# Reordering the superblocks of a fused attention, gated-convolution and MLP kernel

## The chip, the core and the metric

The kernel runs on one core of one Trainium2 chip. The metric is device time in microseconds (us), from the start of the program to its end. Engines are named as in the profile: PE is the matmul engine, PEld its weight loads, DVE the vector engine, ACT the scalar engine, POOL GpSimd, SP the engine whose queue issues all DMAs of this kernel.

## What is computed

Three layers in a row, all in float32, on 8 x 576 rows of 512 values: attention inside chunks of 64 rows (8 heads of 64), a block whose value projection is gated by the sigmoid of a 5-tap causal convolution, and an MLP with a layer norm ahead of it and a residual:

```python
attn = softmax(q_c @ k_c.T / sqrt(64));  x = attn @ v_c          # per chunk and head
gate = sigmoid(sum(conv_w[k] * shift(x, 4 - k) for k in range(5)))
x = (gate * (x @ w_val)) @ w_out
xn = (x - mean(x)) / sqrt(var(x) + 1e-6) * g_ln
out = x + maximum(xn @ w_ch1, 0) @ w_ch2                         # 512 -> 2048 -> 512
```

## The kernel before, in words

A float32 operand is cut into a high part and a low part that PE multiplies at full rate; a product is then three matmuls, high x high, high x low, low x high. ACT makes the high part with a copy, and DVE or POOL makes the low part with a subtraction (`high_low`, L475; `relu` in `ff_pair`, L618).

**Attention (about 0 to 260 us).** Units of 256 rows (`NU` = 18). `load_qk(u)` (L78) brings q and k of a unit into one of two buffers, `sc(u)` (L164) makes its scores and at its end loads unit u + 2. The prologue also calls `load_qk(0)`, `(1)` and `(2)` (L664 to L672); `sc(0)` then loads unit 2 a second time into the other buffer, and it is this copy that `sc(2)` reads.

**MLP, first block (about 260 to 400 us).** 512 rows, 16 slices of 128 hidden values: `ff1` makes a slice, `ff2(0, f)` adds its share to four accumulators, in an order written out by hand for PE. Meanwhile the rows of the next 1024 are normalised (`ln_rows`, L404), transposed (`turn_rows`, L427), and turned into the seven right operands of a Strassen product (`right_operands`, L535).

**MLP, four superblocks of 1024 rows (about 400 to 1084 us, `NS` = 4).** A superblock has eight pairs (`NPR`) of hidden slices. `ff_pair` (L596) makes a 2 x 2 block product from seven products (`prod`) in the two PSUM banks `zy` and `x`. A product is 6 matmuls. ACT copies `zy` out (`copy`), DVE adds `x` to the copy (`add`), and four Relus, named by (slice, half), give the tiles `h`. The second matrix of the MLP is applied one pair later: eight *fillings* (`ff2_tile`, L569), 6 matmuls each, stand between the products of the following pair. Fillings 0 to 3 read `h` (0,0) and (1,0) and add into four accumulators over all pairs; fillings 4 to 7 read (0,1) and (1,1), and DVE adds each to `yt` at once. PE's order in a pair is: product 0 (`zy`), 1 (`x`), fillings 0 to 2, product 2 (`zy`), 3 (`x`), filling 3, product 4 (`zy`), fillings 4 and 5, product 5 (`x`), fillings 6 and 7, product 6 (`x`). Relu (1,0) reads `x` after product 6; product 1 of the next pair overwrites `x`.

In the first superblock `make_pair` (L502) also makes the left operands of the next pair, seven parts with four sums on DVE, a copy on ACT and a subtraction on POOL for each part, and writes them to DRAM (`wc`); later superblocks fetch them into a ring of six tiles. In the first pair the only filling is `open_rest` (L960): the last slice of the first block's `ff2`, after which the pools of the superblocks open. In pairs 2 to 5 of the first three superblocks the rows of the next superblock are normalised, and eight transposes follow the pair.

**What sets the order.** On PE the program's order holds in all of this. On ACT, DVE, POOL and SP the compiler's scheduler orders the instructions when the kernel is built: by program order among those that are ready, in its own model of time; on the chip each queue then runs strictly in that order.

## Time and profile before

| | before |
|---|---|
| time, median of 3 runs | 1086.06 us (1085.44 to 1088.45) |
| profiled execution, its own time | 1085.96 us |
| span of the profile | 1084.2 us, 16824 instructions |
| mean granted clock of PE | 0.992 of full |
| PE busy | 1050.2 us, 97% |
| PEld busy | 857.8 us, 79% |
| DVE busy | 672.2 us, 62% |
| ACT busy | 499.4 us, 46% |
| POOL busy | 60.2 us, 6% |
| DMA | 156.31 MB, mean 144 GB/s |

The span is the time from the first to the last profiled instruction; the execution's own time has 1.8 us around it. Busy time is a sum over one engine's instructions. Matmuls are pipelined and their ends are modelled, so that a row of six matmuls reads 1.52 us while the next group starts 1.36 us after it; a short stall of PE is therefore read from starts, or from the waits of the weight loads, and not from PE's busy share. The page's chain of work that ended last is 85% PE.

### The profile page before, as it was taken

How to read it: one execution, taken by the hardware profiler on the slowest of the kernel's cores; microseconds unless marked ns; L12 is line 12 of the kernel's file. 1: busy time of each engine (PE TensorE's matmuls, PEld its weight loads, DVE VectorE, ACT ScalarE, POOL GpSimd, SP SyncE). 2: the span in 40 equal slices, each digit the busy share in tenths (PEclk: the TensorE clock that was granted, in tenths of full speed). 3: DMA queues.
4: the chain of work that ended last, by engine and by line, in shares of the span. 5: the costliest groups of instructions: out<-in, count | busy, mean ns of one | idle time of the engine just before them, and what ended most of it. 6: DMA issues, size and time to landing. Idle time of an engine off the chain costs nothing.

```text
span 1084.2 us, 16824 instructions
## 1 busy us (share of the span) xinstructions
PE 1050.2 (97%) x6778; PEld 857.8 (79%) x6778; DVE 672.2 (62%) x1098; ACT 499.4 (46%) x872; POOL 60.2 (6%) x88
## 2 busy tenths in 40 slices
PE   4899999999999997999999999999999999999998
PEld 4578888888787886888878888887888888888887
DVE  5899999997958884555566344357344438333434
ACT  5777776766858754254432234333233423222211
POOL 1300000000000033222100000000000000000000
PEclk9899999999989999999999999999999999999999
DMA  9534434412389835334427334325432324522202
GB/s 382 215 134 157 146 135 151 147 60 79 136 264 312 289 133 197 114 120 155 156 93 237 98 97 136 99 96 181 149 114 100 102 84 142 188 80 95 86 31 78
DMA packets 58724, 156.31 MB, mean 144 GB/s; under 512 B 5758, under 2 KB 13974, under 8 KB 56214
## 3 DMA queue, kind: packets, MB, share of 16 engines
q1 hardware_dynamic: 58646, 155.23, 41.4%
q8 instruction: 53, 0.87, 0.3%
q14 instruction: 25, 0.20, 0.1%
HBM read 117.46 MB, written 37.75 MB: 143 GB/s over the span
## 4 chain that ended last, share of the span: by engine, by line
PE 85%; DVE 8%; DMA 2%; ACT 2%; issue 1%; POOL 0%; SPq 0%; ACTq 0%; POOLq 0%
PE acc L583 16%; PE x L609 16%; PE psf L583 15%; PE zy L609 10%; PE pso L334 8%; PE psv L334 8%; PE acc L469 4%; PE psh L334 3%; PE sc L174 2%; PE x L249 2%; DVE h L621 2%; DVE cg L303 1%; PE pst L432 1%; PE pst L217 1%; DMA raw<-in_moe_w_ch 1%
## 5 line engine op out<-in xcount | busy, mean ns | idle before, releaser
L629 DVE TENSOR_TENSOR c<-x,c 128x512 f32<-128x512 f32 x96 | 66.3, 690 | 235.1 <-ACT c L625 179.3
L583 PE MATMUL acc<-w,h 128*128 128x512 f32 x768 | 185.4, 391 | 0.0
L583 PE MATMUL psf<-w,h 128*128 128x512 f32 x768 | 184.3, 389 | 0.0
L583 PEld LDWEIGHTS acc<-w,h 128*128 128x128 f32 x768 | 145.1, 189 | 30.5
L583 PEld LDWEIGHTS psf<-w,h 128*128 128x128 f32 x768 | 144.2, 188 | 29.9
L609 PE MATMUL x<-t,wc 128*128 128x512 f32 x576 | 146.5, 390 | 3.4 <-DVE c L629 3.4
L625 ACT ACTIVATE c<-zy 128x512 f32<-128x512 f32 x96 | 58.0, 604 | 186.7 <-PE zy L609 186.6
L609 PEld LDWEIGHTS x<-t,wc 128*128 128x128 f32 x576 | 108.0, 188 | 26.6 <-DVE c L629 4.3
L620 ACT ACTIVATE h<-c 128x512 fp32r<-128x512 f32 x96 | 60.6, 631 | 135.7 <-DVE c L629 135.1
L588 DVE TENSOR_TENSOR yt<-psf,yt 128x512 f32<-128x512 f32 x128 | 88.2, 691 | 23.5 <-PE psf L583 20.7
L303 DVE SCALAR_TENSOR_TENSOR cg<-xf,cw,cg 128x516 f32<-128x516 f32 (+1 forms) x136 | 100.4, 752 | 3.0
L609 PE MATMUL zy<-b,wc 128*128 128x512 f32 x384 | 98.6, 392 | 0.0
L609 PEld LDWEIGHTS zy<-b,wc 128*128 128x128 f32 x384 | 71.2, 188 | 14.2
L621 DVE SCALAR_TENSOR_TENSOR h<-c,h 128x512 fp32r<-128x512 f32 x96 | 68.0, 708 | 13.4 <-ACT h L620 13.1
L334 PE MATMUL pso<-oh,gh 128*128 128x512 f32 x144 | 58.9, 409 | 1.7 <-ACT gh L370 1.7
L477 POOL TENSOR_TENSOR wc<-raws,wc 128x256 fp32r<-128x256 f32 x56 | 45.4, 833 | 247.5 <-ACT wc L476 238.1
L334 PE MATMUL psv<-xh,vh 128*128 128x512 f32 x144 | 58.6, 407 | 0.0
L334 PE MATMUL pso<-oh,gl 128*128 128x512 f32 x144 | 57.4, 399 | 0.8 <-DVE gl L373 0.7
L334 PE MATMUL pso<-ol,gh 128*128 128x512 f32 x144 | 57.1, 396 | 0.0
L334 PE MATMUL psv<-xl,vh 128*128 128x512 f32 x144 | 56.3, 391 | 0.0
L334 PE MATMUL psv<-xh,vl 128*128 128x512 f32 x144 | 56.3, 391 | 0.0
L620 ACT ACTIVATE h<-x 128x512 fp32r<-128x512 f32 x32 | 19.1, 598 | 80.0 <-PE x L609 80.0
(112 smaller groups left out, 1508.7 us busy)
## 6 DMA issues: line engine op xcount, KB each, us to landing
wc<-wc SPq DMA_DIRECT2D x112, 512.0 KB, 3.2
qkr<-in_qk SPq DMA_DIRECT2D x19, 1024.0 KB, 7.1
raw<-in_moe_w_ch SPq DMA_DIRECT2D x32, 512.0 KB, 4.9
vr<-in_v SPq DMA_DIRECT2D x18, 512.0 KB, 4.1
yd<-y SPq DMA_DIRECT2D x36, 256.0 KB, 2.0
out<-yt SPq DMA_DIRECT2D x36, 256.0 KB, 3.6
yr<-yd SPq DMA_DIRECT2D x32, 256.0 KB, 3.7
yt<-yd SPq DMA_DIRECT2D x32, 256.0 KB, 3.6
```

The source lines that it names most:

```text
L174: nc.tensor.matmul(out=ps[CH * c:CH * c + CH, par, g, :], lhsT=qt[r0:r0 + CH, hp, cs], rhs=kt[r0:r0 + CH, hp, cs], start=True, stop=True,)
L303: last_tap[j] = nc.vector.scalar_tensor_tensor(out=o, in0=xf[j][:, f, i:i + n], scalar=cw[:, i * CT + f:i * CT + f + 1], in1=o, op0=ALU.mu ...
L334: nc.tensor.matmul(out=ps, lhsT=lt, rhs=rh, start=(i == 0), stop=(i == n - 1))
L469: nc.tensor.matmul(out=acc[t], lhsT=lt, rhs=rh, start=(f == 0 and i == 0), stop=(f == NF - 1 and i == 2))
L477: eng.tensor_tensor(out=lo, in0=a, in1=hi, op=ALU.subtract)
L583: nc.tensor.matmul(out=ps, lhsT=lt, rhs=rh, start=(g == 0 and k == 0 and (first or half)), stop=(g == 1 and k == 2 and (last or half)),)
L588: nc.vector.tensor_tensor(out=yt[i], in0=ps, in1=yt[i], op=ALU.add)
L609: nc.tensor.matmul(out=ps, lhsT=lt, rhs=rh, start=(start and c == 0 and i == 0), stop=(c == 1 and i == 2), skip_group_check=True)
L620: nc.scalar.activation(out=t[:, 0, :], in_=src, func=ACTF.Relu)
L621: nc.vector.scalar_tensor_tensor(out=t[:, 1, :], in0=src, scalar=0.0, in1=t[:, 0, :], op0=ALU.max, op1=ALU.subtract)
L625: nc.scalar.activation(out=t, in_=zy, func=ACTF.Copy)
L629: nc.vector.tensor_tensor(out=t, in0=x, in1=t, op=ALU.add)
```

## The change

- `sc(0)` no longer loads unit 2 of q and k; the prologue's copy is the one that is read.
- In pairs that are `late` (pairs 0, 1, 6, 7 of the first three superblocks, all pairs of the last) filling 7 runs after product 6. In all pairs but the first, Relu (1,1) stands last in the program.
- The tiles `h` get six slots of their own, numbered in turn, in place of five that rotate; the tiles `c` get three buffers in place of two; the ring's two extra tiles (`wx`) open earlier, on the other side of memory.
- `open_rest` is cut into four fillings, one for each 128 rows. The first pair's DVE and ACT instructions get a fixed order, with the parts of pair 1 among them. The subtractions of the parts of pairs 0 and 1 go from POOL to DVE. Copies, adds and Relus of the first superblock's pairs 0 and 1 get high priority.
- The ACT instructions of pair 2's `make_pair` are queued behind the first pair's last Relu on ACT, and the DVE instructions of `ln_rows` behind the last Relu on DVE of the pair before (`issue_after`: an order in the queue, not a wait).

```diff
@@ -175,7 +175,7 @@
                         out=ps[CH * c:CH * c + CH, par, g, :], lhsT=qt[r0:r0 + CH, hp, cs], rhs=kt[r0:r0 + CH, hp, cs],
                         start=True, stop=True,
                     )
-        if u + 2 < NU:
+        if 0 < u < NU - 2:
             load_qk(u + 2)
 
     def mx(u):
@@ -456,19 +456,19 @@
 
     acc = {}
 
-    def ff2(j, f):
-        a, b = hh.pop((j, f))
+    def ff2(j, f, ts=range(BLK // P)):
+        a, b = hh[j, f]
         h2, l2 = w2s[f]
         if f == 0:
             for t in range(BLK // P):
                 acc[t] = p2["acc"].tile([P, DM], F32, tag=f"acc{t}", name="acc")
-        for t in range(BLK // P):
-            ts = slice(t * P, (t + 1) * P)
-            ops = [(a[:, ts], h2), (a[:, ts], l2), (b[:, ts], h2)]
+        for t in ts:
+            tt = slice(t * P, (t + 1) * P)
+            ops = [(a[:, tt], h2), (a[:, tt], l2), (b[:, tt], h2)]
             for i, (lt, rh) in enumerate(ops):
                 nc.tensor.matmul(out=acc[t], lhsT=lt, rhs=rh, start=(f == 0 and i == 0), stop=(f == NF - 1 and i == 2))
         if f == NF - 1:
-            for t in range(BLK // P):
+            for t in ts:
                 nc.vector.tensor_tensor(out=yt0[:, t, :], in0=acc.pop(t), in1=yt0[:, t, :], op=ALU.add)
                 nc.sync.dma_start(out=rows(-1, t)[1], in_=yt0[:, t, :])
 
@@ -499,7 +499,7 @@
                 nc.sync.dma_start(out=x, in_=a_dram[2 * p + f].rearrange("p (c w) -> p c w", c=2))
         raws[p] = t
 
-    def make_pair(p):
+    def pair_parts(p, eng):
 
         base = 7 * p
         for k in range(7):
@@ -512,17 +512,22 @@
 
         def high_low_of(k, a):
             n, m = divmod(base + k, 2)
-            high_low(wtiles[n][:, m, 0, :], wtiles[n][:, m, 1, :], a, nc.gpsimd)
+            high_low(wtiles[n][:, m, 0, :], wtiles[n][:, m, 1, :], a, eng)
             if m == 1:
                 nc.sync.dma_start(out=w1c[n], in_=wtiles[n].bitcast(F32))
 
-        high_low_of(0, a12)
-        nc.vector.tensor_tensor(out=s3, in0=a11, in1=a21, op=ALU.subtract)
-        nc.vector.tensor_tensor(out=s1, in0=a21, in1=a22, op=ALU.add)
-        nc.vector.tensor_tensor(out=s2, in0=s1, in1=a11, op=ALU.subtract)
-        nc.vector.tensor_tensor(out=s4, in0=a12, in1=s2, op=ALU.subtract)
-        for k, a in enumerate((a11, s1, s2, s4, s3, a22)):
-            high_low_of(k + 1, a)
+        def sums():
+            nc.vector.tensor_tensor(out=s3, in0=a11, in1=a21, op=ALU.subtract)
+            nc.vector.tensor_tensor(out=s1, in0=a21, in1=a22, op=ALU.add)
+            nc.vector.tensor_tensor(out=s2, in0=s1, in1=a11, op=ALU.subtract)
+            nc.vector.tensor_tensor(out=s4, in0=a12, in1=s2, op=ALU.subtract)
+
+        parts = [lambda k=k, a=a: high_low_of(k, a) for k, a in enumerate((a12, a11, s1, s2, s4, s3, a22))]
+        return parts[:1] + [sums] + parts[1:]
+
+    def make_pair(p, eng=nc.gpsimd):
+        for fn in pair_parts(p, eng):
+            fn()
 
     def fetch(s, n):
         t = ring_tile(s * len(w1c) + n)
@@ -593,12 +598,18 @@
             nc.vector.tensor_tensor(out=y, in0=ps, in1=y, op=ALU.add)
             nc.sync.dma_start(out=rows(s, i)[1], in_=y)
 
+    last_relu = last_act = None
+    hslot = iter(range(4 * NS * NPR))
+
     def ff_pair(s, p, fill):
 
         zy = ps_d.tile([P, BLK], F32, tag="d", name="zy")
         x = ps_d.tile([P, BLK], F32, tag="d", name="x")
         h = {}
         first = s == 0 and p == 0
+        held = last_act
+        late = s + 1 == NS or not 2 <= p < 6
+        early = tc.high_priority if s == 0 and p < 2 else ExitStack
 
         def prod(ps, k, nm, start):
             g = (s * NPR + p) * 7 + k
@@ -607,55 +618,96 @@
                 cs = slice(c * P, (c + 1) * P)
                 for i, (lt, rh) in enumerate(((w[:, 0, cs], b[:, 0, c]), (w[:, 0, cs], b[:, 1, c]), (w[:, 1, cs], b[:, 0, c]))):
                     nc.tensor.matmul(out=ps, lhsT=lt, rhs=rh, start=(start and c == 0 and i == 0), stop=(c == 1 and i == 2), skip_group_check=True)
-            if k == 2 and s == 0 and p + 1 < NPR:
-                make_pair(p + 1)
-                if 0 < p < NPR - 2:
+            if k == 2 and s == 0 and 0 < p < NPR - 1:
+                with tc.issue_after(held.ins) if p == 1 else ExitStack():
+                    make_pair(p + 1)
+                if p < NPR - 2:
                     load_pair(p + 2)
             n = g // 2 + NR
             if g % 2 and len(w1c) <= n < NS * len(w1c):
                 fetch(*divmod(n, len(w1c)))
 
         def relu(key, src):
-            t = h[key] = p2["hr"].tile([P, 2, BLK], F32R, tag="h", name="h")
-            nc.scalar.activation(out=t[:, 0, :], in_=src, func=ACTF.Relu)
-            nc.vector.scalar_tensor_tensor(out=t[:, 1, :], in0=src, scalar=0.0, in1=t[:, 0, :], op0=ALU.max, op1=ALU.subtract)
+            nonlocal last_relu, last_act
+            t = h[key]
+            with early():
+                last_act = nc.scalar.activation(out=t[:, 0, :], in_=src, func=ACTF.Relu)
+                last_relu = nc.vector.scalar_tensor_tensor(out=t[:, 1, :], in0=src, scalar=0.0, in1=t[:, 0, :], op0=ALU.max, op1=ALU.subtract)
+
+        def tiles():
+            for key in ((0, 0), (0, 1), (1, 1), (1, 0)) if first else ((0, 0), (0, 1), (1, 0), (1, 1)):
+                h[key] = p2["hr"].tile([P, 2, BLK], F32R, tag=f"h{next(hslot) % 6}", name="h")
 
         def copy():
             t = p2["c"].tile([P, BLK], F32, tag="c", name="c")
-            nc.scalar.activation(out=t, in_=zy, func=ACTF.Copy)
+            with early():
+                nc.scalar.activation(out=t, in_=zy, func=ACTF.Copy)
             return t
 
         def add(t):
-            nc.vector.tensor_tensor(out=t, in0=x, in1=t, op=ALU.add)
+            with early():
+                nc.vector.tensor_tensor(out=t, in0=x, in1=t, op=ALU.add)
 
         def run(a, b):
             for fn in fill[a:b]:
                 fn()
 
-        prod(zy, 0, "b21", True)
-        c = copy()
-        prod(x, 1, "b11", True)
-        add(c)
-        if not first:
+        if first:
+            with tc.manual_schedule(engines={mybir.EngineType.DVE, mybir.EngineType.Activation}):
+                prod(zy, 0, "b21", True)
+                c = copy()
+                prod(x, 1, "b11", True)
+                parts = pair_parts(1, nc.vector)
+                parts[0]()
+                add(c)
+                run(0, 2)
+                prod(zy, 2, "t1", True)
+                parts[1]()
+                parts[2]()
+                d = copy()
+                prod(x, 3, "t2", False)
+                parts[3]()
+                prod(zy, 4, "b22", False)
+                e = copy()
+                add(e)
+                run(2, 4)
+                tiles()
+                relu((0, 0), c)
+                prod(x, 5, "t3", False)
+                add(d)
+                parts[4]()
+                prod(x, 6, "t4", False)
+                relu((1, 0), x)
+                parts[5]()
+                parts[6]()
+                relu((0, 1), e)
+                parts[7]()
+                relu((1, 1), d)
+        else:
+            tiles()
+            prod(zy, 0, "b21", True)
+            c = copy()
+            prod(x, 1, "b11", True)
+            add(c)
             relu((0, 0), c)
-        run(0, 3)
-        if first:
-            relu((0, 0), c)
-        prod(zy, 2, "t1", True)
-        d = copy()
-        prod(x, 3, "t2", False)
-        run(3, 4)
-        prod(zy, 4, "b22", False)
-        c = copy()
-        add(c)
-        relu((0, 1), c)
-        run(4, 6)
-        prod(x, 5, "t3", False)
-        add(d)
-        relu((1, 1), d)
-        run(6, 8)
-        prod(x, 6, "t4", False)
-        relu((1, 0), x)
+            run(0, 3)
+            prod(zy, 2, "t1", True)
+            d = copy()
+            prod(x, 3, "t2", False)
+            run(3, 4)
+            prod(zy, 4, "b22", False)
+            c = copy()
+            add(c)
+            relu((0, 1), c)
+            run(4, 6)
+            prod(x, 5, "t3", False)
+            add(d)
+            run(6, 7 if late else 8)
+            prod(x, 6, "t4", False)
+            relu((1, 0), x)
+            if late:
+                run(7, 8)
+            relu((1, 1), d)
         return [lambda i=i: ff2_tile(s, p, h, i) for i in range(2 * HB)]
 
 
@@ -950,23 +1002,26 @@
         if f == NF - 4:
             s_1.close()
             p2["xb"] = ctx.enter_context(tc.tile_pool(name="xb", bufs=1, reuse_waits="tile"))
-            p2["c"] = ctx.enter_context(tc.tile_pool(name="pc", bufs=2, reuse_waits="tile"))
+            p2["c"] = ctx.enter_context(tc.tile_pool(name="pc", bufs=3, reuse_waits="tile"))
+            p2["wx"] = ctx.enter_context(tc.tile_pool(name="p2w", bufs=1, reuse_waits="tile"))
             right_operands()
     load_pair(0)
     load_pair(1)
-    make_pair(0)
+    make_pair(0, nc.vector)
     load_pair(2)
 
-    def open_rest():
-        ff2(0, NF - 1)
+    def open_rest(t):
+        ff2(0, NF - 1, [t])
+        if t < BLK // P - 1:
+            return
         s_0.close()
-        p2["hr"] = ctx.enter_context(tc.tile_pool(name="p2r", bufs=5, side="right", reuse_waits="tile"))
-        p2["wx"] = ctx.enter_context(tc.tile_pool(name="p2w", bufs=1, side="right", reuse_waits="tile"))
+        p2["hr"] = ctx.enter_context(tc.tile_pool(name="p2r", bufs=1, side="right", reuse_waits="tile"))
         p2["yt"] = ctx.enter_context(tc.tile_pool(name="pyt", bufs=2, reuse_waits="tile"))
 
-    fill = [open_rest]
+    fill = [lambda t=t: open_rest(t) for t in range(BLK // P)]
     for s in range(NS):
         for p in range(NPR):
+            before = last_relu
             fill = ff_pair(s, p, fill)
             if p == 0:
                 load_yt(s, 1)
@@ -974,7 +1029,10 @@
                 load_yt(s, 0)
             if s + 1 < NS and 2 <= p < 6:
                 i = 2 * (p - 2)
-                turn_rows(ln_rows([load_rows(s + 1, i + k) for k in range(2)]), i)
+                ys_next = [load_rows(s + 1, i + k) for k in range(2)]
+                with tc.issue_after(before.ins):
+                    ln_rows(ys_next)
+                turn_rows(ys_next, i)
         if s + 1 < NS:
             right_operands()
     for fn in fill[HB:] + fill[:HB]:
```

## Rows read from the trace of the kernel before

**Rows 1.** Waits, weight loads: who waited for whom: us in total, times, longest.

```profile
PEld x L609 <- DVE h L621: 11.9, 19, 2.9
...
PEld x L609 <- DVE c L629: 4.3, 2, 3.1
```

**Rows 2.** Windows between fillings: length, busy us of PE, PEld, DVE, ACT, POOL, clock.

```profile
549.13:570.05 20.92, 20.70 (x91) 16.82 (x91) 14.26 (x18) 8.63 (x12) 0.00 (x0) 1.00 0.26 93
...
590.80:611.54 20.74, 20.69 (x91) 16.81 (x91) 7.49 (x11) 4.29 (x7) 0.00 (x0) 1.00 0.47 157
611.54:632.84 21.30, 21.30 (x100) 17.73 (x99) 7.96 (x12) 6.25 (x15) 0.00 (x0) 1.00 0.32 102
```

**Rows 3.** Timeline, end of an ordinary pair: start us, us, what [idle before <-releaser].

```profile
961.65 2.88 PE L583 MATMUL psf<-w,h 128*128 128x512 f32 x12
...
961.85 0.69 DVE L629 TENSOR_TENSOR c<-x,c 128x512 f32<-128x512 f32 x1 [0.67 <-PE x L609]
...
964.37 1.52 PE L609 MATMUL x<-t,wc 128*128 128x512 f32 x6
...
965.73 1.52 PE L609 MATMUL zy<-b,wc 128*128 128x512 f32 x6
965.92 0.60 ACT L620 ACTIVATE h<-x 128x512 fp32r<-128x512 f32 x1 [2.72 <-PE x L609]
966.56 0.69 DVE L621 SCALAR_TENSOR_TENSOR h<-x,h 128x512 fp32r<-128x512 f32 x1 [1.30 <-ACT h L620]
...
967.30 1.65 PE L609 MATMUL x<-b,wc 128*128 128x512 f32 x6
```

**Rows 4.** Timeline of the first superblock's first pair, all engines.

```profile
398.88 1.52 PE L609 MATMUL zy<-b,wc 128*128 128x512 f32 x6
...
401.33 0.42 DVE L521 TENSOR_TENSOR raws<-raws 128x256 f32<-128x256 f32 x1
...
403.19 2.48 DVE L472 TENSOR_TENSOR yt<-acc,yt 128x512 f32<-128x512 f32 x4
...
408.44 1.32 ACT L476 ACTIVATE wc<-raws 128x256 fp32r<-128x256 f32 x4
408.57 1.19 DVE L621 SCALAR_TENSOR_TENSOR h<-c,h 128x512 fp32r<-128x512 f32 x1 [2.90 <-ACT h L620]
...
411.22 1.65 PE L609 MATMUL x<-t,wc 128*128 128x512 f32 x6 [2.66 <-DVE c L629]
...
416.05 0.69 DVE L410 BATCH_NORM_STATS2 s<-yr 128x6 f32<-128x512 f32 x1 [2.45 <-DMA yr<-yd]
...
419.15 2.28 PE L609 MATMUL x<-b,wc 128*128 128x512 f32 x6 [2.44 <-DVE h L621]
...
421.23 5.31 PE L583 MATMUL acc<-w,h 128*128 128x512 f32 x18
```

**Rows 5.** Windows before the first pair and after its waits.

```profile
380.00:400.00 20.00, 20.00 (x90) 16.55 (x89) 17.91 (x19) 12.23 (x20) 8.16 (x8) 1.00 0.29 108
...
420.00:422.00 2.00, 2.00 (x6) 1.61 (x5) 0.86 (x3) 0.07 (x1) 0.00 (x0) 0.50 0.78 242
```

**Rows 6.** Timeline, end of the first superblock and the pair after it.

```profile
562.99 0.68 DVE L629 TENSOR_TENSOR c<-x,c 128x512 f32<-128x512 f32 x1
...
565.29 1.52 PE L609 MATMUL x<-t,wc 128*128 128x512 f32 x6
...
573.93 0.68 DVE L629 TENSOR_TENSOR c<-x,c 128x512 f32<-128x512 f32 x1
...
575.33 1.52 PE L609 MATMUL x<-t,wc 128*128 128x512 f32 x6
```

**Rows 7.** Groups: the subtractions on POOL: xcount | busy us, mean ns | idle before.

```profile
L477 POOL TENSOR_TENSOR wc<-raws,wc 128x256 fp32r<-128x256 f32 x56 | 45.4, 833 | 247.5 <-ACT wc L476 238.1
```

**Rows 8.** Waits of the score products; timeline row of the third unit's.

```profile
PE sc L174 <- DMA qkr<-in_qk: 5.8, 1, 5.8
...
23.25 1.99 PE L174 MATMUL sc<-qkr 64*64 64x64 f32 x64
```

## The prediction

> **What bounds the kernel now.** I read the busy shares first. TensorE is busy 97% of the span, so a change can only win where its queue is interrupted, and a stall of a few tenths of a microsecond is hidden inside that share, since the ends of matmuls are modelled. The view to trust for that is the wait table of the weight loads: in the superblock stage the loads for `x` waited 19 times for the low half of a Relu, 11.9 us together, and twice for the add into `c` [rows 1]. Next come windows cut from one pair's first filling to the next one's: 20.75 us for an ordinary pair, 20.92 where a superblock ends, 21.30 where eight transposes are added [rows 2]. Twelve matmuls follow each other in 2.72 us (961.65 to 964.37 in [rows 3]), 0.2267 each; a pair has 42 of products and 48 of fillings, 90 x 0.2267 = 20.40. So an ordinary pair loses **0.35 us**, a superblock's last **0.52**, and a pair with transposes nothing (21.30 - 20.40 = 0.90 for the eight).
>
> [rows 3] shows where the 0.35 goes. After the last product (L609, 964.37, nominally over at 965.73) PE goes on with the next pair's `zy`, 1.36 us. Product 1 writes the `x` bank, which Relu (1,0) still reads: ACT starts 0.19 after the product, 0.60, then DVE 0.69 to 967.25, PE at 967.30. Nominal was 967.09: 0.21 late, and 0.14 more because the weight load no longer lies under a matmul. DMA, ACT and POOL hold nobody up here.
>
> The second place is the first pair [rows 4]. From its first product (398.88) to the fillings of pair 1 (421.23) are 22.35 us for 66 matmuls, 14.96 at full rate: 7.39 lost. Two products wait for adds, the first at 411.22 for 2.66, and the one at 419.15 waits 2.44 for the Relu's low half. Right after that the granted clock is 0.50 at 420 to 422, 1.2 of the 2.4 GHz [rows 5], and the 18 matmuls of that filling take 5.31 us against 4.08 for 18 at 0.2267 plus 0.16 for the modelled end: 1.07 more. Together **8.46 us**.
>
> **Part by part.**
>
> *Last filling behind the last product* (`late` pairs: 0, 1, 6, 7 of the first three superblocks, all of the fourth). The 19 waits are 15 ordinary boundaries, 3 superblock ends, and the first pair's. PE now has a filling (6 matmuls, 1.36) and `zy` (1.36) between the last product and product 1: 2.72 against the 1.52 that the Relu takes (0.19 + 0.60 + 0.04 + 0.69). The wait goes: 15 x 0.35 = **5.25**. What is late next: the last product comes 1.36 earlier, so the add of `d` before it (961.85, 0.69) must be over within 1.36 of product 5's end at 961.65; it ends at 962.54, 0.89 after, slack 0.47. The moved filling takes its yt add (0.69 on DVE) along; it is ready 1.36 + 0.19 after the product, when the Relu's low half is just over. In the next superblock's first pair the last fillings also carry output DMAs on SP, with yt loads and `wc` fetches queued behind; these slip by 1.36, against a ring of 6 tiles, 12 products ahead. No cost.
>
> At a superblock's end DVE also makes the right operands. There the add of `d` runs from 562.99 to 563.67; the last product starts at 565.29, and could now 1.36 earlier, at 563.93: slack 0.26 [rows 6]. In the next pair the add of `c` ends at 574.61 for a product at 575.33 [rows 6]; PE comes 0.5 earlier, slack 0.2. I take 0.4 of the 0.52: 3 x 0.4 = **1.2**; bounds: all (1.56) and a loss as large, if DVE misses both.
>
> *Six numbered `h` slots, Relu (1,1) last.* Tile n sits in slot n mod 6, so (1,1) takes the slot of the previous pair's (0,1), which the last filling reads: it must wait for that filling. In ordinary pairs some 10 us lie before its first reader (10 groups of 1.36, less its own turn of 3). After the very last pair it has none: fillings follow at once. ACT can start 1.36 + 0.19 after the product, 0.63; the fourth matmul of the next filling wants it at 1.36 + 0.68 = 2.04 and gets it at 2.2; the low half, behind a yt add, is some 0.2 late again. With uncovered loads about **-0.45**; bounds 0 and -1.5 (whole ACT + DVE turn, 0.63 + 0.69, uncovered).
>
> *First pair in a fixed order.* ACT's queue held four copies of weight parts (408.44, 1.32) before the copy that product 5's add needs; POOL's subtractions stretch DVE's Relu at 408.57 to 1.19 (0.69 elsewhere); the normalisation's 0.69 at 416.05 and its like lie before the low half that PE waits for at 419.15 [rows 4]. The diff takes all three away and pays for it: seven subtractions for pair 0 and seven for pair 1 go from POOL to DVE. No row has this form on DVE; the nearest, the sums 128x256, take 0.42 (401.33 in [rows 4]), POOL's own 0.83 is the other end [rows 7]. I take 0.45 with its gap: it is the same engine, type and size. DVE is busy 17.91 of 380 to 400 [rows 5]; seven more, 3.2, make it some 2.5 late at 399, while the first add is due at 2.9.
>
> Counting from the first product as 0: `zy` to 1.36, `x` to 2.72; DVE: part 0 to 2.9, add of `c` to 3.6, two accumulator adds (4 took 2.48: 0.62 each, [rows 4]) to 4.9, four sums to 6.7, two parts to 7.6. PE: two fillings to 4.08, product 2 to 5.44, 3 to 6.8, 4 to 8.16, two fillings to 9.52. Copy of `zy` 8.35 to 8.95, add to 9.67: product 5 at 9.7 (0.2 late, 0.14 uncovered), over at 11.2. DVE then has two accumulator adds to 10.9, a Relu low half to 11.6 and only then the add of `d`, to 12.3: product 6 waits 1.1, runs 12.35 to 13.85. `zy` of pair 1 to 15.2, product 1 after the Relu at 15.4, fillings at 16.9. Against 22.35: 5.45. PE's longest rest is 1.1, where it was 2.66 and 2.44, so I let the clock stay up: 1.07. **6.5** together. Bounds: 8.46 (nothing lost) and 2.4, if DVE runs 3 us later than this and the clock falls again.
>
> The Trainium skill, Perfetto Trace Analysis, section Optimizing Scalar/DVE Operations, speaks against this part: work moved between GpSimd and VectorE may not help, since they share a read port. By it this term would stand at its lower bound; the stretched Relu at 408.57 would be the sharing it means.
>
> *Normalisation held back* elsewhere: its DVE steps now start behind the previous pair's last Relu, some 20 us before the transposes that read them. Queued behind it is nothing that PE needs. 0.
>
> *make_pair(2) behind the first pair's last ACT Relu*: pair 2's parts then have all of pair 1, 20 us, for 7 x 0.83 on POOL. 0.
>
> *q and k of unit 2 once.* One transfer of 1 MB less. The only wait of a score product for q and k is the first, 5.8, before that; the third unit's products start at 23.25 with no wait on PE [rows 8]. 0; a transfer that PE never waits for gives back nothing, and one fewer adds no wait.
>
> **Sum** against the profiled execution's 1085.96 (span 1084.2 and 1.8 around it; the median of the runs shown is 1086.06, so the same): 5.25 + 1.2 + 6.5 - 0.45 = 12.5, **1073.5 us**.
>
> **The rivals.** *The first pair hardly gains*: DVE with 14 more operations comes later than I count, PE rests over 2 us, the clock falls. 2.4 in place of 6.5 and 1 of slips: 1085.96 - 5.25 - 1.2 - 2.4 + 0.45 + 1 = 1078.6. For: DVE nearly full before. Against: by the count DVE is free from 7.6 to 8.95, ahead of product 5.
>
> *The last filling brings nothing.* If the yt add of that filling sits before the Relu's low half in DVE's queue, the low half runs from 2.24 to 2.93 after the product, and product 1, due at 2.72, is as late as now (0.26 + 0.14). Only the first pair is left: 1085.96 - 6.5 + 0.45 = 1079.9. Against: the low half is ready at 0.83, the add at 1.55, and in [rows 3] DVE's queue follows readiness. The Trainium skill, Perfetto Trace Analysis, section Optimization Strategy, says that a bubble repeating in the same place can mean too few buffers; `x` has no new bank here, so by that rule this rival is the outcome.
>
> *Slower.* Relu (1,1) now waits for the last filling. If its ACT instruction is queued ahead of Relu (1,0), which frees `x`, ACT stands until 1.55 after the product, then runs 0.63 and 0.60 to 2.8; DVE has the yt add, (1,1) and (1,0) to 3.6, and product 1 comes 0.95 late and 0.14 uncovered, 1.09 where it was 0.35: 15 x 0.74 + 3 x 0.57 = 12.8 lost. With the first pair's 6.5 and the end's 0.45: 1085.96 + 12.8 - 6.5 + 0.45 = 1092.7. It decides as soon as the turn is over 0.7 a pair. Against: the program names (1,0) first, and it is ready first.
>
> **How the numbers follow.** The forecast 0.63, hardly a gain in the first pair 0.14, no gain from the filling 0.11, slower 0.07, something between worth under 0.3% 0.05. About 0.3%, 3.3 us, is what a measurement can tell. Faster 0.63 + 0.14 + 0.10 = 0.87, same 0.05, slower 0.08. The range: low end with all stalls gone, 1085.96 - 8.46 - 5.25 - 1.56 = 1070.7, so 1070.5; high end past both rivals that still gain, with a little over 1 us for the superblock ends: 1081.
>
> **What will show it.** Windows from filling to filling: 20.4 in the late pairs (20.75 if the second rival is right, 21.5 if the slower one), 21.3 where transposes run. Waits of `x` for the Relu's low half: one or two left out of 19. From the first product to pair 1's fillings 17 us, one wait of about 1.1 at product 6, a granted clock of 1.00 behind it. At the end a wait for Relu (1,1) of some tenths. The first 60 us unchanged but for one transfer. I am wrong if a pair in the steady stretch keeps a wait, if the superblock ends grow over 20.92, or if the first pair's DVE queue runs far behind its products.

## The result, and the profile after

The kernel after takes **1072.84 us** (median of 4 runs, 1072.4 to 1076.57) against 1086.04 beside it: a ratio of 0.9882, interval 0.9855 to 0.9909. The prediction was 1073.5. The profiled execution took 1072.57, its span is 1070.8, 13.4 less than before; PE is busy 97% as before.

The answer to [rows 1], the waits of the weight loads. The 19 waits for a Relu's low half have become one of 0.5 us:

```profile
PEld x L620 <- DVE c L649: 2.1, 3, 1.2
...
PEld x L620 <- DVE h L635: 0.5, 1, 0.5
```

The answer to [rows 2], windows from filling to filling with the same columns: the last pair of the first superblock, the first of the second, an ordinary pair and one with transposes.

```profile
541.23:561.63 20.40, 20.40 (x91) 16.89 (x90) 13.55 (x17) 8.19 (x12) 0.00 (x0) 1.00 0.30 101
561.63:582.11 20.48, 20.48 (x92) 16.82 (x90) 15.47 (x21) 6.30 (x9) 0.00 (x0) 1.00 0.66 220
582.11:602.51 20.40, 20.40 (x92) 16.90 (x90) 8.69 (x15) 4.29 (x7) 0.00 (x0) 1.00 0.50 166
602.51:623.80 21.29, 21.29 (x99) 17.72 (x98) 9.25 (x23) 7.96 (x18) 0.00 (x0) 1.00 0.30 99
```

An ordinary pair takes 20.40, 90 matmuls at full rate, where it took 20.75, and so does a superblock's last (20.92); the pair behind that takes 20.48, and 21.3 with transposes is left. The answer to [rows 3], the timeline at the end of such a pair:

```profile
598.43 1.52 PE L588 MATMUL psf<-w,h 128*128 128x512 f32 x6
598.63 0.60 ACT L634 ACTIVATE h<-x 128x512 fp32r<-128x512 f32 x1 [4.75 <-PE x L620]
599.26 0.69 DVE L635 SCALAR_TENSOR_TENSOR h<-x,h 128x512 fp32r<-128x512 f32 x1 [1.30 <-ACT h L634]
...
599.79 1.52 PE L620 MATMUL zy<-b,wc 128*128 128x512 f32 x6
...
601.15 1.52 PE L620 MATMUL x<-b,wc 128*128 128x512 f32 x6
```

The last filling stands at 598.43. The Relu's low half ends at 599.95, 1.2 us before product 1 wants `x` at 601.15, and no row of PE here has a wait.

The answer to [rows 4], the timeline of the first pair:

```profile
398.21 1.52 PE L620 MATMUL zy<-b,wc 128*128 128x512 f32 x6
...
406.57 0.60 ACT L644 ACTIVATE c<-zy 128x512 f32<-128x512 f32 x1 [1.76 <-PE zy L620]
...
407.94 1.65 PE L620 MATMUL x<-t,wc 128*128 128x512 f32 x6
...
409.63 0.69 DVE L649 TENSOR_TENSOR c<-x,c 128x512 f32<-128x512 f32 x1
...
410.38 1.66 PE L620 MATMUL x<-t,wc 128*128 128x512 f32 x6 [0.79 <-DVE c L649]
...
413.45 1.66 PE L620 MATMUL x<-b,wc 128*128 128x512 f32 x6
...
414.95 4.24 PE L588 MATMUL acc<-w,h 128*128 128x512 f32 x18
```

And the window of [rows 5] (length, busy us of PE, clock, DMA):

```profile
420.00:422.00 2.00, 2.00 (x11) 1.00 0.28 29
```

From the first product to pair 1's fillings 16.74 us where it was 22.35; the fillings take 4.24 where they took 5.31, at a clock of 1.00 (2.4 GHz), which holds in every window of 2 us from 390 to 424. Below, *the stretch* is the time from the first product to pair 1's fillings. Two new small waits came with the change. In pair 1, product 5 is late by 0.31 (PEld at 427.36), because pair 3's sums on DVE, the last one stretched to 0.84 beside POOL, are queued ahead of an add (timeline):

```profile
425.65 1.66 POOL L477 TENSOR_TENSOR wc<-raws,wc 128x256 fp32r<-128x256 f32 x2 [1.12 <-ACT wc L476]
425.86 0.84 DVE L523 TENSOR_TENSOR raws<-raws 128x256 f32<-128x256 f32 x1
426.63 0.68 DVE L649 TENSOR_TENSOR c<-x,c 128x512 f32<-128x512 f32 x1
...
427.36 1.23 PEld L620 LDWEIGHTS x<-t,wc 128*128 128x128 f32 x6 [0.43 <-DVE c L649]
```

And the timeline behind the very last pair:

```profile
1054.52 7.27 PE L588 MATMUL psf<-w,h 128*128 128x512 f32 x30
1054.72 0.60 ACT L634 ACTIVATE h<-x 128x512 fp32r<-128x512 f32 x1 [4.75 <-PE x L620]
...
1055.40 0.63 ACT L634 ACTIVATE h<-c 128x512 fp32r<-128x512 f32 x1
1056.07 0.69 DVE L635 SCALAR_TENSOR_TENSOR h<-c,h 128x512 fp32r<-128x512 f32 x1
1056.67 1.47 DVE L593 TENSOR_TENSOR yt<-psf,yt 128x512 f32<-128x512 f32 x2
1057.41 3.95 PEld L588 LDWEIGHTS psf<-w,h 128*128 128x128 f32 x18 [0.42 <-DVE yt L593]
...
1061.62 5.60 PE L588 MATMUL acc<-w,h 128*128 128x512 f32 x24
```

Relu (1,1) started on ACT at 1055.40, right behind Relu (1,0). The fillings behind it nevertheless took 7.10 us for 30 matmuls (6.80 at full rate), since the first yt add, which frees their PSUM bank, stands behind that Relu's low half on DVE (1056.07 to 1056.67); PE's next weight load waits 0.42 us for it (1057.41).

Where the 13.4 us are, from starts of the same products in both traces (a pair's mark is the start of its product 2):

| stretch | predicted | measured |
|---|---|---|
| first product to pair 1's fillings | 5.45 | 22.35 - 16.74 = 5.61 |
| those fillings at the higher clock | 1.07 | 5.31 - 4.24 = 1.07 |
| 3 x (superblock end and the boundary behind it) | 3 x (0.4 + 0.35) = 2.25 | 2.38 |
| 11 further boundaries | 3.85 | 3.83 |
| the first superblock's pair 1 to pair 2 | 0.35 | 0.04 |
| the end | -0.45 | 28.33 - 28.52 = -0.19 |
| start of the first product | 0 | 398.88 - 398.21 = 0.67 |
| sum | 12.5 | 13.4 |

### The profile page after: what moved, and what is told of

Read it like the earlier page. It is cut to its first block, busy times and chain, and to the rows that moved or that the text cites. A ratio compares the mean times of both kernels' runs of the same rounds, so it can differ in the third digit from the quotient of the medians.

```text
span 1070.8 us, 16849 instructions
## 1 busy us (share of the span) xinstructions
PE 1043.3 (97%) x6778; PEld 856.7 (80%) x6778; DVE 675.0 (63%) x1112; ACT 497.6 (46%) x872; POOL 46.9 (4%) x74
## 4 chain that ended last, share of the span: by engine, by line
PE 91%; DVE 4%; DMA 2%; ACT 2%; issue 1%; SPq 0%; ACTq 0%; DVEq 0%
PE psf L588 16%; PE acc L588 16%; PE x L620 16%; PE zy L620 12%; PE psv L334 8%; PE pso L334 8%; PE acc L469 3%; PE psh L334 3%; PE x L249 2%; PE sc L174 2%; PE pst L217 2%; DMA raw<-in_moe_w_ch 1%; PE pst L432 1%; DVE cg L303 1%; PE psc L324 1%; PE x L283 1%
## 5 line engine op out<-in xcount | busy, mean ns | idle before, releaser
L588 PE MATMUL psf<-w,h 128*128 128x512 f32 x768 | 187.5, 389 | 0.0
L620 PE MATMUL x<-b,wc 128*128 128x512 f32 x192 | 48.8, 390 | 0.1
```

The source lines that it names most:

```text
L588: nc.tensor.matmul(out=ps, lhsT=lt, rhs=rh, start=(g == 0 and k == 0 and (first or half)), stop=(g == 1 and k == 2 and (last or half)),)
L620: nc.tensor.matmul(out=ps, lhsT=lt, rhs=rh, start=(start and c == 0 and i == 0), stop=(c == 1 and i == 2), skip_group_check=True)
```

## The experiments

**The kernel after without the last filling's move.**

```diff
-        late = s + 1 == NS or not 2 <= p < 6
+        late = False
```

> The changed kernel with no late pairs: filling 7 goes back ahead of product 6 everywhere, all else stays. My theory: the waits of product 1 for the Relu's low half come back, 18 of them, pairs take 20.75 us instead of 20.40, superblock ends 20.9, and the 0.3 us at the very end go: 15 x 0.35 + 3 x 0.5 - 0.3 = 6.4 us slower at most, 1078 to 1079. Rival, that the repeated wait was a lack of buffers and six slots for h cured it: no change, 1072.8, pairs at 20.40.

1081.16 us (10 runs, 1079.34 to 1083.68), above the 1078 to 1079 expected; ratio to the kernel before 0.9948, interval 0.9934 to 0.9962. 18 more waits for the low half are there than in the kernel after (19 against 1). From pair 0's mark to the last pair's it takes 648.34 where the kernel after takes 639.99, and the end 28.23 where it took 28.52: the move is worth 8.06 us in this kernel, and it costs 0.29 at the end. That is 2 more than it gains over the kernel before (2.38 + 3.83 + 0.04 - 0.19 = 6.06). Without the move this kernel is slower than the kernel before at three boundaries, 21.13 twice and 21.52 where they were 20.75 (0.39 of the 21.52 is pair 1's late product 5), and at the superblock ends, 41.84 over two pairs where it was 41.67. The timeline of one of the three:

```profile
604.30 1.28 DVE L410 BATCH_NORM_STATS2 s<-yr 128x6 f32<-128x512 f32 x2
...
605.50 0.67 DVE L635 SCALAR_TENSOR_TENSOR h<-x,h 128x512 fp32r<-128x512 f32 x1
...
606.23 1.66 PE L620 MATMUL x<-b,wc 128*128 128x512 f32 x6 [0.43 <-DVE h L635]
```

The statistics of the held normalisation come in between: they are held behind the pair's Relu (1,1), and without the move the scheduler queues Relu (1,1), which is ready first, ahead of Relu (1,0). So two parts of the change lean on each other.

**Relu (1,1) ahead of Relu (1,0) on ACT**, the rival by which the change would have been slower:

```diff
             prod(x, 6, "t4", False)
-            relu((1, 0), x)
             if late:
                 run(7, 8)
-            relu((1, 1), d)
+                relu((1, 1), d)
+                with tc.issue_after(last_act.ins):
+                    relu((1, 0), x)
+            else:
+                relu((1, 0), x)
+                relu((1, 1), d)
```

> The kernel after, with ACT's Relu (1,1) ahead of Relu (1,0) in all pairs whose last filling stands behind product 6 (the first pair aside). It tests the rival by which the change would have been slower: that the read of the slot by the last filling holds up ACT's queue. Theory A (Relu (1,1) waits for the half of the last filling that reads its slot, 0.68 us behind the start of the filling, and Relu (1,0) with its low half then ends behind the next pair's product 0): each of 18 boundaries gets 0.3 to 0.7 us longer, 20.40 becomes 20.7 to 21.1, the time 5 to 13 us more than the 1072.8 of the kernel after, 1078 to 1086. Theory B (there is room for both in the 2.7 us that filling and product 0 take): 20.40 stays and the time too.

1092.24 us in one execution, slower than the kernel before (1084.83 beside it) and above both theories. Every ordinary late boundary takes 0.90 more, 21.30 for 20.40, in place of the 0.3 to 0.7 of theory A, a superblock's end with the boundary behind it 2.49 more (43.37 for 40.88); 18 more waits for the low half are there (19 against 1). The timeline of one of them:

```profile
582.66 1.52 PE L588 MATMUL psf<-w,h 128*128 128x512 f32 x6
583.54 0.63 ACT L634 ACTIVATE h<-c 128x512 fp32r<-128x512 f32 x1 [5.43 <-PE psf L588]
...
584.20 0.69 DVE L635 SCALAR_TENSOR_TENSOR h<-c,h 128x512 fp32r<-128x512 f32 x1 [2.01 <-ACT h L634]
584.81 0.68 DVE L593 TENSOR_TENSOR yt<-psf,yt 128x512 f32<-128x512 f32 x1
585.41 0.68 DVE L635 SCALAR_TENSOR_TENSOR h<-x,h 128x512 fp32r<-128x512 f32 x1
...
586.14 1.65 PE L620 MATMUL x<-b,wc 128*128 128x512 f32 x6 [0.61 <-DVE h L635]
```

ACT waited for the filling (582.66) until 583.54, then came (1,1), then (1,0); on DVE (1,1)'s low half and a yt add stood ahead of (1,0)'s. Product 1 was due at 585.38 (two groups of 1.36 behind 582.66). So the mechanism of that rival is real and only the order in ACT's queue keeps it away. Two details differ from its price. ACT waited 0.88 us from the filling's start, not the whole 1.36 + 0.19: only the first three matmuls of that filling read the slot, and 3 x 0.2267 + 0.19 is 0.87. And the turn on DVE, 1.9 us for three instructions, was the longer part.

**Subtractions of pairs 0 and 1 back on POOL**, in the kernel after:

```diff
-                parts = pair_parts(1, nc.vector)
+                parts = pair_parts(1, nc.gpsimd)
...
-    make_pair(0, nc.vector)
+    make_pair(0, nc.gpsimd)
```

> The changed kernel with the subtractions of the parts of pairs 0 and 1 back on POOL, the order of the first pair as changed. My theory (POOL stretches DVE operations that read two tiles, 1.19 for 0.69 before): the first pair's stretch from its first product to pair 1's fillings, 16.74 us, grows by 0.5 to 1.5. The rule that moving between the two engines doesn't help: it stays at 16.7 or shrinks, since DVE is relieved of 7 x 0.42 us there.

1075.68 us in one execution. First product to pair 1's fillings: 16.75, against 16.74. With the order fixed, the move to DVE neither gains nor costs anything there; nearly all that this execution has above 1072.8 lies ahead of the first product (401.13, not 398.21).

**No order fixed by hand**, in the kernel after:

```diff
-            with tc.manual_schedule(engines={...DVE, ...Activation}):
+            with ExitStack():
```

> The changed kernel without the fixed order of the first pair's DVE and ACT instructions (the scheduler orders them), parts on DVE as changed. If the order is what gained: the stretch of 16.74 us grows by 2 us or more and the granted clock may fall behind it. Rival, that it was POOL's absence and the held-back normalisation: it stays within 0.7 us of 16.74.

1073.4 us in one execution, the first pair again 16.74, and pair 1's new wait is gone: 20.40 to the next mark where the kernel after has 20.71. So neither of the two edits on which the prediction put the 6.5 us is needed as long as the other stands. No run takes both out of the kernel after, so either may stand in for the other. The other parts of the change that reach the first pair are the storage (three `c`, `wx` on the other side, six `h` slots), the priorities, the halved filling, the normalisation held back, and pair 2's parts queued on ACT behind the first pair's last Relu. Four kernels take these apart, three of them built on the kernel before.

**The normalisation held back, alone** (kernel before):

```diff
...
-                turn_rows(ln_rows([load_rows(s + 1, i + k) for k in range(2)]), i)
+                ys_next = [load_rows(s + 1, i + k) for k in range(2)]
+                with tc.issue_after(before.ins):
+                    ln_rows(ys_next)
+                turn_rows(ys_next, i)
```

> The kernel before, with one part of the change alone: the normalisation of the next superblock is held behind a low half of Relu of the pair before. Marks are starts of product 2 of the pairs. In the kernel before the first pair takes 22.06 us from mark to mark; 2.44 of it is the wait of its last product for Relu (1,0)'s low half, which stood on DVE behind statistics that had waited for their load, and 2.66 the wait of product 5 for an add whose copy started late. Theory A (the normalisation made the second of these two waits): it falls to some 0.3, the first pair to about 20.0, and the wait of product 5 stays at about 2.7; the time about 2 us less. Theory B (it is covered, as my prediction priced it, at 0): the first pair stays within 0.3 of 22.06.

The timeline of its first pair, products 5, 6 and pair 1's product 1:

```profile
412.48 2.43 PE L611 MATMUL x<-t,wc 128*128 128x512 f32 x6 [2.67 <-DVE c L632]
...
415.69 2.93 PE L611 MATMUL x<-t,wc 128*128 128x512 f32 x6 [0.78 <-DVE c L632]
...
420.50 1.53 PE L611 MATMUL x<-b,wc 128*128 128x512 f32 x6
```

The wait before pair 1's product 1 (2.44 in [rows 4]) is gone: at 420.50 it stands behind product 0 with no gap. From mark to mark the pair takes 20.37 (22.06), near theory A, but by another sum: the clock fell early here (0.50 at 414 to 416), products 5 and 6 took 2.43 and 2.93 us, so that the stretch is only 0.62 shorter (21.73), and the clock was up again for the fillings, 1.07. So this run does not show what the hold is worth. In the second trace under *q and k* below nothing is held, the clock falls equally early, and that wait is gone as well, with a stretch of 21.74. The time, 1085.56 in one execution against 1084.71 beside it, shows no gain.

**The storage alone** (kernel before, three `c` buffers, `wx` on the left):

```diff
-            p2["c"] = ctx.enter_context(tc.tile_pool(name="pc", bufs=2, ...
+            p2["c"] = ctx.enter_context(tc.tile_pool(name="pc", bufs=3, ...
+            p2["wx"] = ctx.enter_context(tc.tile_pool(name="p2w", bufs=1, ...
...
-        p2["wx"] = ctx.enter_context(tc.tile_pool(name="p2w", bufs=1, side="right", ...
```

> The kernel before, with its order as it is and with the storage of the change alone: three buffers for the copies in place of two, and the ring tiles of the weights on the left. Theory A (the third copy started late because a buffer for it was missing): product 5's wait falls from 2.66 us to about 1.5, since the copy can start at the end of product 4 and only the copy, the add and their hand-overs are left; the first pair falls from 22.06 to about 21, and the wait of 2.44 before its last product stays, since the normalisation isn't held here. Theory B (the order of the instructions on ACT and DVE, which the change fixes by hand, made it): product 5's wait stays at about 2.7 and the first pair at about 22.

Both theories fell: product 5's wait grew to 4.66, the stretch to 24.34 and the time to 1089.19 in one execution. From the timeline:

```profile
408.68 1.27 DVE L410 BATCH_NORM_STATS2 s<-yr 128x6 f32<-128x512 f32 x2
...
414.00 0.58 ACT L625 ACTIVATE c<-zy 128x512 f32<-128x512 f32 x1
...
415.48 2.93 PE L609 MATMUL x<-t,wc 128*128 128x512 f32 x6 [4.66 <-DVE c L629]
```

With another layout the scheduler put the normalisation even earlier, on DVE ahead of the low half and the add and on ACT ahead of the copy, which came at 414.00 for a product that was over at 410.66. The clock was 0.50 from 414 on.

**Both together:**

> The kernel before with both: three buffers for the copies, the ring tiles on the left, and the normalisation held. No order is fixed, nothing is moved between POOL and DVE, the first pair's filling is in one piece. Theory A (the two waits have these two causes): the first pair falls to 18.0 to 18.9 us (22.06, less 1.1 of product 5's wait, less 2.1 of the last product's), and what is left to the 16.74 of the kernel after is the half of the filling that the change moves between products 4 and 5 (1.36). Theory B (order and moved work are needed): 20 or more.

1085.69 us in one execution, 1084.71 beside it. From the timeline, a low half of Relu, products 5 and 6, and the window behind them (length, busy us of PE, clock, DMA):

```profile
410.72 1.19 DVE L624 SCALAR_TENSOR_TENSOR h<-c,h 128x512 fp32r<-128x512 f32 x1 [2.06 <-ACT h L623]
...
412.57 2.00 PE L611 MATMUL x<-t,wc 128*128 128x512 f32 x6 [1.85 <-DVE c L632]
...
415.35 2.93 PE L611 MATMUL x<-t,wc 128*128 128x512 f32 x6 [0.78 <-DVE c L632]
```

```profile
414.00:416.00 2.00, 1.22 (x4) 0.50 0.25 96
```

From mark to mark 19.54 us, above the 18.0 to 18.9 of theory A and below the 20 of theory B; the stretch is 20.90. Against the storage alone, which also ran at the low clock there, the hold makes product 5's wait 1.85 where it was 4.66, and the stretch 3.44 shorter. What is missing to theory A is the clock again, 0.50 (1.2 GHz) at 414 to 416: from product 5 to product 1 the starts are 2.78, 2.73 and 2.50 apart, where the next kernel, with no other waits there and a clock of 1.00, has 2.44, 1.51 and 1.59. That is 2.47. And the add for product 5 starts at 411.83, although its copy is over at 411.35: ahead of it on DVE stands a low half that took 1.19 beside POOL's subtractions (410.72; 0.69 in the next kernel).

**The filling in one piece** (kernel after, free order):

```diff
-                run(0, 2)
+                run(0, 4)
...
-                run(2, 4)
```

> The kernel after without the order fixed by hand, and with the first pair's filling in one piece between products 1 and 2, as in the kernel before. The same kernel with the filling in two halves took 16.74 us from mark to mark. Theory A (the second half, 1.36 us of PE's work, stands where product 5 has to wait for its add in any case): the first pair as a whole, from the start of its product 0 to that of pair 1's product 0, gets 1.36 longer, since product 2 starts 1.36 later and product 5 waits that much longer. Theory B (the place of the filling doesn't matter because the copies are in time): no more than 0.3 longer, with a wait of product 5 below 0.5.

Product 5 in its timeline:

```profile
409.29 1.65 PE L620 MATMUL x<-t,wc 128*128 128x512 f32 x6 [1.41 <-DVE c L649]
```

1073.74 us in one execution; the stretch is 18.14 us where the halves give 16.74: 1.40 more, as theory A said. Product 5 starts 1.57 behind the nominal end of product 4, for a copy and an add that nothing delays (0.19 + 0.60 + 0.03 + 0.69, and the hand-over); the second half of the filling, 1.36, covers nearly all of it.

**The kernel after with the normalisation free:**

```diff
-                with tc.issue_after(before.ins):
-                    ln_rows(ys_next)
+                ln_rows(ys_next)
```

> The kernel after, without the edge that holds the next superblock's normalisation behind a low half of Relu; its place on DVE and ACT is then free. The first pair keeps its fixed order, so the first place it can take is pair 1. Theory A (it fills the first gap it finds and stands ahead of the adds and low halves that PE waits for, as in the kernel before with the new storage alone, where product 5's wait grew to 4.66 us): pair 1's mark, 20.71 us in the kernel after, grows by 0.3 to 2 us. Theory B (DVE has slack there, and my price of 0 holds): 20.71 within 0.1. The later pairs, 20.40 and 21.3, are the same by both.

Theory A, near its upper end: pair 1's mark is 22.40 where it was 20.71, 1.69 more, the first pair 16.73; 1076.88 us in one execution. In the timeline of pair 1 the statistics are ahead of the add that product 6 needs:

```profile
432.40 1.29 DVE L410 BATCH_NORM_STATS2 s<-yr 128x6 f32<-128x512 f32 x2 [0.57 <-DMA yr<-yd]
433.60 0.67 DVE L649 TENSOR_TENSOR c<-x,c 128x512 f32<-128x512 f32 x1
...
434.33 1.66 PE L620 MATMUL x<-t,wc 128*128 128x512 f32 x6 [1.42 <-DVE c L649]
```

**q and k of unit 2 once** (kernel before):

```diff
-        if u + 2 < NU:
+        if 0 < u < NU - 2:
```

> The kernel before with the single load of unit 2's q and k alone. My prediction says 0: no wait of PE for q and k goes, so all marks of PE stay within 0.2 us and the time at 1086. The trace of after suggests a second theory: pv at 60.00 us is at 59.57 there and the first superblock product at 398.21 instead of 398.88; if the load does it (by another order of ACT's queue around 29 us, since the order is made in a model of time in which that data comes sooner), this kernel shows the same, 0.4 us at 60 and 0.4 to 0.7 us in all. If it is noise between executions, both marks stay where they were before.

> The kernel before with the one edit on q and k, whose first look took 1082.28 us, below each of the runs of the kernel before. Theory A (my price: the second load is hidden, 0): ratio to the kernel before 1.000 within 0.001. Theory B (ACT and SP get another order behind it, and the work ahead of the superblocks gets shorter by 1 to 4 us): ratio 0.996 to 0.999.

1082.28 us in one execution; then 1084.05 as the median of 12 runs against 1084.83 of 17, ratio 0.999, interval 0.998 to 1.000. It is worth between nothing and 2 us. The mark at 60.00 us is at 58.41 in both traces, but it lies anywhere from 58.42 to 60.05 in the kernels above that are built on the kernel after, which all have this edit. The two traces, of the same kernel, show the first pair in two ways, the first one's timeline ahead of the second's:

```profile
409.57 1.65 PE L609 MATMUL x<-t,wc 128*128 128x512 f32 x6 [2.66 <-DVE c L629]
...
417.19 1.65 PE L609 MATMUL x<-b,wc 128*128 128x512 f32 x6 [2.13 <-DVE h L621]
...
418.69 4.24 PE L583 MATMUL acc<-w,h 128*128 128x512 f32 x18
```

```profile
410.03 2.24 PE L609 MATMUL x<-t,wc 128*128 128x512 f32 x6 [2.66 <-DVE c L629]
...
416.91 0.68 DVE L621 SCALAR_TENSOR_TENSOR h<-x,h 128x512 fp32r<-128x512 f32 x1
418.05 1.53 PE L609 MATMUL x<-b,wc 128*128 128x512 f32 x6
...
419.42 4.24 PE L583 MATMUL acc<-w,h 128*128 128x512 f32 x18
```

In the first the clock stays up and product 1 waits 2.13 for the normalisation; in the second product 5 runs at a lower clock, the products behind it come later, and the wait is gone, although the normalisation stands ahead of the low half (416.91) here as well. The stretches are 21.46 and 21.74, and 22.35 in the kernel before, where the clock fell only behind the waits.

**A version with the two small waits taken away**: the kernel after with a free order, and the very last pair not late.

```diff
-        late = s + 1 == NS or not 2 <= p < 6
+        late = p < NPR - 1 if s + 1 == NS else not 2 <= p < 6
```

> The kernel after, without the order fixed by hand in the first pair, and with the very last pair's fillings in front of product 6 as in the kernel before. Theory A: pair 1's mark is 20.40 (20.71 in the kernel after), the stretch from the last pair's product 2 to the end 28.2 (28.52), the first pair 16.7; 0.6 us in all, so about 1072.2 with a ratio of 0.987 to 0.989 to the kernel before. Theory B (the last pair's 0.3 belongs to its later position, not to the filling's): the last stretch stays at 28.5, and only 0.3 is gained.

1070.94 us (4 runs, 1070.76 to 1072.19), ratio 0.9876, interval 0.9861 to 0.9891. Its marks are those of theory A: 16.74, 20.40, and 28.23 at the end, 0.6 us less than the kernel after. The intervals of the two kernels overlap, so the times alone don't tell them apart; the rest of the difference, 1.26, lies ahead of the first product (396.95).

## Why the prediction came out right, step by step

**The last filling** was right in mechanism and size: 6.25 us of boundaries where 6.45 were forecast, and without the move the waits come back. The three superblock ends with the boundaries behind them kept 2.38 of the 2.61 that stood there; I had taken 2.25. What it missed is the one boundary of 0.04: in pair 1 product 5 now waits for an add behind pair 3's sums, a queue that I had not followed there; the free order gives the 0.31 back.

The Trainium skill, Perfetto Trace Analysis, section Optimization Strategy, led to the rival that nothing would be gained without another buffer. The bubble did repeat at one place, and here 19 waits became one with the two PSUM banks as they were; with the added buffers for `c` and `h` but without the move, 18 more waits are there.

**The first pair** was right in its sum, partly by luck, and its reasons were incomplete. The step that failed is the one that says the fixed order and the move to DVE take the ACT copies, the POOL stretching and the normalisation away: without the one or without the other the stretch stays at 16.74 or 16.75. That both are worth nothing is not shown, since both away at once was not tried. The 5.61 us come from these, as far as the runs separate them:
- to product 5, 2.61: the storage, 2.66 to 1.85 of wait (with the normalisation held), 0.81; the half of the filling over the wait that is left, about 1.4; the remaining 0.4 between the kernel before with storage and hold (1.85) and the kernel after in one piece (1.41). In the former the add stands behind a low half stretched to 1.19 beside POOL, in the latter the subtractions are on DVE. This is the stretching that the prediction named, at 0.4 us; whether the move, the priorities, the order on ACT or the `h` slots cure it was not separated.
- from there on, 3.00, read from the two timelines and not isolated by a run: 2.42 for pair 1's product 1, whose low half no longer stands behind the normalisation, and 0.58 of that product at the lower clock.

The luck is the clock's. In the execution of the kernel before that the forecast was read from, the clock fell behind the waits. In the first trace under *q and k*, with the same order in the first pair, it stayed up, and stretch and fillings took 21.46 + 4.24 = 25.70 us, where the kernel before has 22.35 + 5.31 = 27.66 and the kernel after 20.98. Measured from there, the gain is 4.72 and not 6.68.

My simulation by hand of the fixed order gave 16.9 all the same, since it followed the chain that both orders share (copy, add, product): it had product 5 at 9.7 behind the first product, and it came at 9.73. One wait in it was mis-sized: product 6 waits 0.79, not 1.1. DVE's queue is not in the way; the add starts at 409.63 as soon as product 5 is over, and 0.79 is the bare turn, the same in every kernel here.

The Trainium skill, same page, section Optimizing Scalar/DVE Operations, said that moving work from GpSimd to VectorE may not help. The experiment agrees as long as the order is fixed (16.75 against 16.74); my conclusion from it, that the term would then stand at its lower bound, doesn't follow, as the gain didn't hang on that move alone.

**The normalisation at 0** was wrong: I priced what is queued behind it when it is held, and not where it goes when it isn't. The hold saves 1.69 us in the kernel after and 3.44 in the kernel before with the new storage; in the kernel before as it is, its worth is not shown. In the sum this was hidden, since I had booked the wait for the normalisation under the fixed order. The edge on pair 2's parts, also priced at 0, was not tested alone.

**The clock** came back as forecast (1.07), but it isn't a fixed price of these waits. With the same order it fell to 0.50 behind them (kernel before), in the middle of them, or not at all. Why it falls in one execution and not in another stays open.

**The end**, -0.45: it cost 0.19 to 0.29, by another wait than I had named. Relu (1,1) is not held by the last filling as a whole, and what PE waits for is a PSUM bank.

**Slower** was a fair rival: its order of the queue gives 1092.24 where I had worked out 1092.7, with terms that miss in opposite directions. The single boundary is dearer than before by 0.55 where I said 0.74, a superblock's end with the boundary behind it by 1.70 where I said 1.31.

**q and k** at 0 stands within 2 us. The start of the first product, 0.67 earlier, can't be put down to it: between kernels that are the same up to there it lies from 396.95 to 400.79.

## What to carry to other kernels

A stall on the matmul engine at a fixed place of a loop can be covered by moving independent matmuls of the same loop behind the product whose result is awaited; count first whether what moved back still ends before its own reader, and which instruction is first in the queue that frees the bank. A scheduler that fills gaps by readiness can put background work ahead of a critical chain when some storage comes free, as it did here: hold that work behind a named instruction before giving the chain more buffers. When several edits are aimed at one stall, take each away on its own, and those aimed at the same wait together: here each of two was worth nothing while the other stood, and one that was priced at nothing was worth 1.69 us. A stall's price read from one execution holds for that execution's clock; take a second trace before booking it.

## What the runs showed of the hardware

- With the first pair's order unchanged, the granted clock stayed at 1.00 through waits of 2.66, 0.79 and 2.13 us in one execution, and in another of the same kernel it fell behind the first wait (0.50 at 412 to 416). At the lower clock 6 matmuls took 2.93 us; since others waited for DVE at that time, the pair as a whole differed by only 0.28.
- A DVE instruction of 0.69 us took 1.19 while POOL worked; where that instruction stood ahead of an awaited add, the add came 0.48 us behind the end of its copy. With all the subtractions of two pairs on POOL and the order fixed, the instruction stretched to 1.21 stood off the path, and the first pair was no slower.
- With Relu (1,1) first on ACT, its slot was released by the last matmul that read it, the third, and not by the end of the group of six (1.36 us): ACT started 0.88 us after the group's start.
